# Two attentions with a gate: numerators in halves, inverses sent a head at a time, a tile as the constant, zeros from DRAM

## The chip, the cores and the metric

The kernel runs on one core of one Trainium2 chip. The metric is the device time of one launch in microseconds (us). The kernel before took 1031.26 us, the median of 3 runs (1030.42 to 1031.37). Everything is written for this one shape, and all of it is one launch.

## What is computed

Two attentions over the same 2048 rows of x (448 columns, 16 heads of 28) are mixed by a gate. A is linear attention: a learned feature map with two softmaxes per head, the state kv, the numerators phi_q kv and the denominators phi_q z + 1e-6. B is softmax attention.

```python
# A                                   S = 2048, D = 448, H = 16, Dh = 28
q, k, v = split(x @ A_wqkv)           # heads of 28
pq, pk  = q @ w_phi, k @ w_phi        # per head
phi_q   = concat(softmax(pq), softmax(-pq))        # 56 features; phi_k alike
kv, z   = phi_k.T @ v, sum(phi_k, rows)
num     = phi_q @ kv
den     = (phi_q @ z) + 1e-6
a       = merge_heads(num / den) @ A_wo
# B
b       = merge_heads(softmax(q @ k.T * Dh**-0.5) @ v) @ B_wo
g       = sigmoid((x * gate_w).sum(-1, keepdims=True))
out     = g * a + (1 - g) * b
```

## The kernel before, in words

All sums are kept in float32. A product whose inputs need more than the fast format holds is split into a high and a low part and done in three passes, so that one 128x448 product of 448 inputs is 11 or 12 matmuls on PE. The rows are handled in 16 tiles of 128 (`NT`). The order of the work on PE, DVE, ACT and POOL is written by hand; all the DMAs the text speaks of are issued by one queue, SP, in the order in which they are placed there, and a transfer that has to wait for something holds up all that stand behind it on SP. SP also waits, before each transfer, for the one eight places ahead of it.

The kernel has three stretches. Up to about 176 us, PE computes the projections and the state `KV` of A; from about 346 us to the end it is softmax attention B. Between them lies the part that the change touches: the **loop over q** from 0 to 26, in which A's outputs are made while the values of B are projected. One round holds, in this order and as far as they exist for that q:

- the product `pq` of tile q (lines 116, 11 matmuls), its features (`features1`, `features2`) and their transposition into `fT` (`turn`, line 541, DVE);
- `norm2` early (q = 19), the projection `poa` of `out_a` (line 116, three tiles of 448 columns being 12 matmuls each; ACT scales the result into `ga` at line 593, line 594 stores it to DRAM as `gad`);
- `value_b`, the product `pvb` of a tile of B's values (line 116 or 135, 11 matmuls), at q = 2 to 10, 17 and 22 in this loop;
- at q = 6, 10, 14, 18 the **numerators** `numer(n)` of four tiles together (n = 0 to 3; "tile n" below is such a group of four): 128 matmuls of 32x128 at line 552, each on a quarter of rows and a quarter of columns of PE, from `fT` and `KV` into two PSUM tiles `pn_0` and `pn_1`. Each of these 128 is two matmuls in the trace, each with its weight load. Right behind them, `normalize1` copies both to SBUF (`oUa`, ACT, line 413) and sends the rows that hold the denominators to `dena` (line 418, four DMAs);
- `norm2` at q = 7, 11, 15 late in the round, and at q = 19 early: for each half of the tile DVE adds 1e-6 to `dena` (line 424) and takes the reciprocal (line 425), SP sends it to DRAM as `rda` (line 429, two DMAs for each half), and one DMA for each half spreads it to all 128 partitions, 32 for each of four heads, as `rsa` (line 430, 128 partitions of 1024 numbers, 512 KB);
- `normalize3` (line 436, DVE, numerators times inverses, `oUa` x `rsa`) and `normalize4` (line 444 ACT, high part; line 445 DVE or POOL, low part, `oTa`) three and four rounds after the numerators, which feed `out_a`.

From q = 19 on, single units of B's row maxima are strewn in by `tick` (`mx_unit`: matmuls `pmb` and `pmd` at line 295, then ACT line 302 and DVE line 304). At q = 21 the first operand pair of B is set up in `qk` (the memory of `wqA_s`, whose last use is `pq` of tile 15): POOL sets two stacks of 128x2048 to zero and one row to -1 (lines 873 and 874), then SP loads the transposed queries and keys (line 774, from `qkd`) and the row maxima (line 786, from `nm`). The first scores of B use them (line 960).

Of the kernel before, what the change touches and what calls it, by code (L numbers as in the profile page):

```python
# [17 lines left out]
P = 128  # L18
# [5 lines left out]
NG = 4  # L24
# [11 lines left out]
def f32(ap):  # L36
    return ap.bitcast(F32)
# [3 lines left out]
def gated_mix_kernel(ctx, tc, xT, wqkB, wvB, wvA, wkAT, wqAT, phi, woA, woB,  # L41
# [50 lines left out]
    gate = const.tile([P, NT], F32, name="gate")  # L92
    gate1 = const.tile([P, NT], F32, name="gate1")

    w1p = ctx.enter_context(tc.tile_pool(name="w1p", bufs=1, reuse_waits="tile"))
# [70 lines left out]
    acts = []  # L166
    subs = []
    part = mxp.tile([P, NU * 4], F32, name="part", bufs=1)
    nc.gpsimd.memset(part, LOWEST)
# [251 lines left out]
    def normalize2(pool, oU, den, nm, n, eps):  # L421

        if eps:
            nc.vector.tensor_scalar_add(den, den, EPS)
        nc.vector.reciprocal(den, den)
        rd = dr.tile([4, n * 512], F32, tag=f"rd{n}", name=f"rd{nm}", bufs=2)
        rs = pool.tile([P, n, 512], F32, tag="rs", name=f"rs{nm}", bufs=2)
        for k in range(n):
            nc.sync.dma_start(rd[:, k * 512:(k + 1) * 512], den[:, k, :])
        nc.sync.dma_start(rs.rearrange("p n q -> p (n q)"),  # L430
                          rd.unsqueeze(1).to_broadcast([4, 32, n * 512]))
        return oU, rs
# [110 lines left out]

    def numer(n):

        pn = [ps_mx(f"pn{n}_{i}", False) for i in range(2)] if n else pn_next
        for g in range(NG):
            for b in range(2):
                for a in range(4):
                    for c in range(4):  # L550
                        rows, k = slice(32 * a, 32 * a + DH), 2 * g + b
                        nc.tensor.matmul(pn[a // 2][32 * c:32 * c + 32, a % 2, g * P:(g + 1) * P],  # L552
                                         KV[rows, k // 4, k % 4 * P + 32 * c:k % 4 * P + 32 * c + 32],
                                         fT_of[n][rows, :, 2 * (4 * g + c) + b, :],
                                         start=b == 0, stop=b == 1, tile_position=(32 * a, 32 * c),
                                         skip_group_check=True)
        for i in range(2):
            num[n, i] = normalize1(ta, pn[i], f"a{n}_{i}", 2)
# [133 lines left out]
    for n in range(4, NP):  # L692
# [9 lines left out]
        if n == 14:  # L702
            part_loads("wvA", wvA, 450, "wvA")
            nc.sync.dma_start(sel_s, sel)
            for v in vap:
                nc.gpsimd.memset(v[:, :, 28:32], 0.0)
                nc.gpsimd.memset(v[:, :, 28:29], 1.0)
# [138 lines left out]
    for q in range(NT + 11):  # L846
# [23 lines left out]
        if q == 21:  # L870
            w = f32(weights(1, "qk0"))
            for i in range(2):
                nc.gpsimd.memset(w[:, i], 0.0)
            nc.gpsimd.memset(w[0:1, 1], -1.0)
            qst.append(w[:, 0].bitcast(F32R))
# [17 lines left out]
        if q < NT:  # L893
            fq[q] = features1(pq, f"q{q}", nc.gpsimd)
        norm4(q, "B")
        if 1 < q <= NT:
            fq[q - 1] = features2(fq[q - 1], f"q{q - 1}")
# [3 lines left out]
        for u in ((), (q - 3, q - 2), (q - 2,), (q - 2,))[(q - 2) % 4]:  # L901
            if 0 <= u < NT:
                turn(u)
# [6 lines left out]
        if q == NT + 2:  # L910
            bd_s.close()
            vb = [value_tile(0)]
        norm2(q, True)
        if q >= 11:
            out_a((q - 11) // 4, (q - 11) % 4)
        if q in VALUE:
            value_b(VALUE[q], tick if q > NT + 2 else None)
# [3 lines left out]
        if q % 4 == 2 and 6 <= q <= NT + 2:  # L921
            numer(n4)
        if q == NT + 6:
# [415 lines left out]
```

## Time and profile before

One execution was profiled; it took 1032.88 us, of which the profile's span is 1031.1 us and 1.78 us lie around it.

| | before |
|---|---|
| median of 3 runs | 1031.26 us |
| the profiled execution | 1032.88 us |
| its span | 1031.1 us |
| PE matmul, busy | 1003.3 us (97%) |
| PE weight load, busy | 563.5 us (55%) |
| ACT, busy | 794.6 us (77%) |
| DVE, busy | 679.2 us (66%) |
| POOL, busy | 236.6 us (23%) |
| mean granted PE clock | 0.984 |

Times are us from the start of the span. PE is the matmul stream, PEld the weight loads, SPq the queue of SP. In a timeline a row has the start, the busy time, the engine with line, operation, out<-in, and xN for N instructions in a run; in brackets the idle time before it and what ended it. In the chain of work that ended last a row has start and length; "issue" is time in which the engine waited for nothing that the profile shows. In a table of windows each engine's busy time and count come first, then the granted PE clock, the mean busy share of the 16 DMA engines, and GB/s.

### The profile page before, as it was taken

The page shows a single profiled execution, that of the slowest core. Times are in us where ns is not written, and L with a number is a line of the kernel's source. Part 1 is how long each engine was busy: PE and PEld are TensorE (multiplying, and loading weights), DVE is VectorE, ACT ScalarE, POOL GpSimd, SP SyncE. Part 2 cuts the span into 40 slices and gives each one's busy share as a digit, 9 for nine tenths or more (in the row PEclk, how much of TensorE's full clock was granted, in tenths as well). Part 3 has the DMA queues.
Part 4 walks back from the last instruction along what each step waited for, and adds up shares of the span by engine and source line. Part 5 has one row for each costly group of instructions (what it writes and reads, how often), then busy time and mean ns, then how long its engine had stood idle before and what let it go on. Part 6 is the DMA issues. An engine that isn't in the chain of part 4 may idle for free.

```text
span 1031.1 us, 19220 instructions
## 1 busy us (share of the span) xinstructions
PE 1003.3 (97%) x7116; PEld 563.5 (55%) x7116; DVE 679.2 (66%) x1349; ACT 794.6 (77%) x1491; POOL 236.6 (23%) x230
## 2 busy tenths in 40 slices
PE   9999999999966999999999999999999999999998
PEld 8878777888855643333333333333333444454656
DVE  5567777757754668788878888888887444444202
ACT  5456555444433699999999999999999999979682
POOL 1265455656740420201102101012011011011010
PEclk9999999999987999999999999999999999999999
DMA  8975311512225574223444243352342363316141
GB/s 296 311 249 173 112 59 59 178 44 84 90 82 138 174 169 101 55 63 71 83 94 107 61 93 79 87 107 70 78 94 54 87 137 80 104 36 155 51 120 54
DMA packets 73430, 111.80 MB, mean 108 GB/s; under 512 B 20776, under 2 KB 32728, under 8 KB 73208
## 3 DMA queue, kind: packets, MB, share of 16 engines
q1 hardware_dynamic: 73336, 110.57, 39.8%
q8 instruction: 56, 0.92, 0.4%
q14 instruction: 38, 0.31, 0.1%
HBM read 76.04 MB, written 34.08 MB: 107 GB/s over the span
## 4 chain that ended last, share of the span: by engine, by line
PE 92%; DMA 5%; DVE 2%; issue 1%; SPq 0%; ACT 0%; POOL 0%; POOLq 0%; DVEq 0%; ACTq 0%
PE st L1009 27%; PE pv L1108 24%; PE pm L336 8%; PE pqk L116 6%; PE pq L116 4%; PE pk L135 4%; PE pva L135 4%; PE pob L116 3%; PE pmb L295 2%; PE pvb L116 2%; PE poa L116 2%; DMA qk<-nm 2%; DMA rsa<-rda 1%; PE pvb L135 1%; PE pn L552 1%; DMA kst<-qkd 1%
## 5 line engine op out<-in xcount | busy, mean ns | idle before, releaser
L1012 ACT ACTIVATE p<-st 128x512 f32<-128x512 f32 x1020 | 527.8, 642 | 26.4 <-PE st L1009 26.4
L347 DVE TENSOR_REDUCE part<-pm 128x1 f32<-128x512 f32 x450 | 287.4, 685 | 150.5 <-PE pm L336 150.5
L1108 PE MATMUL pv<-p,vb 128*32 128x512 f32 x2048 | 263.7, 603 | 0.0
L340 ACT ACTIVATE rl<-pm 128x512 f32<-128x512 f32 x200 | 124.6, 623 | 14.1 <-PE pm L336 12.4
L336 PEld LDWEIGHTS pm<-kc,qc 28*128 28x128 f32 x800 | 38.3, 182 | 167.6 <-issue 101.4
L436 POOL TENSOR_TENSOR oUb<-oUb,rsb 128x512 f32<-128x512 f32 x15 | 19.3, 1287 | 460.2 <-DMA rsb<-rdb 196.3
L1009 PE MATMUL st<-qk,kst 128*128 128x512 f32 x384 | 116.2, 425 | 0.6 <-DMA kst<-qkd 0.6
L1009 PE MATMUL st<-qst,kst 128*128 128x512 f32 x384 | 114.8, 423 | 0.0
L344 DVE CUSTOM_DVE_ANT_0 rl<-pm,rl 128x512 f32<-128x512 f32 x150 | 102.0, 680 | 0.0
L336 PE MATMUL pm<-kc,qc 28*128 28x512 f32 x800 | 101.3, 495 | 0.0
L1108 PEld LDWEIGHTS pv<-p,vb 128*32 128x32 f32 x2048 | 47.6, 108 | 95.4 <-issue 88.7
L1009 PEld LDWEIGHTS st<-qst,kst 128*128 128x128 f32 x384 | 64.3, 188 | 37.8 <-ACT p L1012 16.5
L1009 PEld LDWEIGHTS st<-qk,kst 128*128 128x128 f32 x384 | 63.9, 188 | 38.6 <-ACT p L1012 17.8
L304 DVE CUSTOM_DVE_ANT_0 rl<-pmb,rl 128x512 f32<-128x512 f32 x88 | 56.5, 679 | 27.0 <-ACT rl L302 26.9
L302 ACT ACTIVATE rl<-pmd 128x1024 f32<-128x1024 f32 x44 | 45.2, 1027 | 28.6 <-PE pmd L295 20.1
L116 PE MATMUL pqk<-XH,wB 128*128 128x512 f32 x192 | 59.8, 399 | 0.0
L116 PE MATMUL poa<-woA_s,oTa 128*128 128x448 f32 x192 | 48.9, 407 | 2.9 <-ACT oTa L444 2.9
L116 PEld LDWEIGHTS poa<-woA_s,oTa 128*128 128x128 f32 x192 | 39.7, 212 | 9.7 <-ACT oTa L444 3.2
L617 ACT CAST ev<-pqk 128x512 fp32r<-128x512 f32 x28 | 16.1, 588 | 36.5 <-PE pqk L116 29.0
L469 ACT ACTIVATE feat<-feat 128x896 f32<-128x896 f32 x32 | 30.6, 956 | 13.5 <-POOL feat L466 13.5
L116 PEld LDWEIGHTS pqk<-XH,wB 128*128 128x128 f32 x192 | 35.3, 188 | 9.0 <-issue 2.2
L116 PE MATMUL pq<-wqA_s,XH 128*128 128x448 f32 x128 | 39.9, 395 | 0.0
(172 smaller groups left out, 1340.8 us busy)
## 6 DMA issues: line engine op xcount, KB each, us to landing
qkd<-ev SPq DMA_DIRECT2D x28, 512.0 KB
qk<-qkd SPq DMA_DIRECT2D x48, 224.0 KB
kst<-qkd SPq DMA_DIRECT2D x48, 224.0 KB
qst<-qkd SPq DMA_DIRECT2D x32, 224.0 KB
od<-oTb SPq DMA_DIRECT2D x48, 112.0 KB
rsa<-rda SPq DMA_DIRECT2D x8, 512.0 KB
rsb<-rdb SPq DMA_DIRECT2D x15, 256.0 KB
kc<-qkd SPq DMA_DIRECT2D x64, 56.0 KB
```

Source lines behind the costliest of these rows:

```text
L116: nc.tensor.matmul(dst, l, r, start=i == 0, stop=i == len(todo) - 1, skip_group_check=mid is not None)
L135: nc.tensor.matmul(dst[:, :n], l, r, start=i == 0, stop=i == len(todo) - 1, skip_group_check=True)
L302: nc.scalar.activation(rl, pd, AF.Relu)
L304: nc.vector.tensor_tensor_reduce(rl[:, i, :], pb[:, i, :], rl[:, i, :], 1.0, LOWEST, ALU.add, ALU.max, part[:, col + i:col + i + 1])
L336: nc.tensor.matmul(pm[j], mxs[("qc", gq)][js, qt * P:(qt + 1) * P], mxs[("kc", g, kb)][js, :], start=True, stop=True, tile_position=(32 * ...
L340: nc.scalar.activation(rl, pm[kb], AF.Relu if kb < 3 else AF.Copy)
L344: nc.vector.tensor_tensor_reduce(r, pm[j], r, 1.0, LOWEST, ALU.add, ALU.max, part[:, col + j:col + j + 1])
L347: nc.vector.tensor_reduce(part[:, col + j:col + j + 1], pm[j], AX.X, ALU.max)
L469: exps.append(lambda: nc.scalar.activation(fx, fx, AF.Exp))
L1009: nc.tensor.matmul(st, kst_of[(gq // NQ, kt // 4)][:, j, (kt % 4) * P:(kt % 4 + 1) * P], qst_of[gq][:, j, :], start=True, stop=True)
L1012: nc.scalar.activation(p, st, AF.Exp, scale=SCALE)
L1108: nc.tensor.matmul(pv[32 * j:32 * j + 32, :], vb[kt // 8][:, kt % 8, 4 * g + j, :], pt[j], start=kt == 0, stop=kt == NT - 1, tile_position ...
```

## The change

The numerators of a tile are issued in two halves of 64 matmuls (`half` 0 and 1: two of the four groups `g` each), and the first half stands ahead of a value product where one exists in that round; the copy and the loads of the denominators stay behind the second half. The constant 1e-6 is added as a tensor, broadcast from a 128x1 tile `eps_s`. Of the two forms of `normalize2`, the one with two halves (A) sends each inverse row with a DMA of its own, 32 partitions of 1024 numbers, four for what was one. The two stacks are no longer cleared by POOL: a small DRAM tile `c_d` with a row of zeros and a row of -1 is filled early (n = 14 of the first stretch), and five DMAs copy from it, four of them into four partitions each, one into one row. Conditions in the diff that are never true (`2 == 0`, `2 == 1`, `() and`) place nothing; `2 == 2` always holds. In the kernel after, lines are 3 to 12 higher.

```diff
--- before.py
+++ after.py
@@ -91,6 +91,8 @@
     z_s = const.tile([P, NT], F32, name="z_s")
     gate = const.tile([P, NT], F32, name="gate")
     gate1 = const.tile([P, NT], F32, name="gate1")
+    eps_s = const.tile([P, 1], F32, name="eps_s")
+    nc.vector.memset(eps_s, EPS)
 
     w1p = ctx.enter_context(tc.tile_pool(name="w1p", bufs=1, reuse_waits="tile"))
     fr_s = ExitStack()
@@ -165,6 +167,7 @@
     nm_of = {}
     acts = []
     subs = []
+    c_d = dr.tile([2, 4096], F32, tag="cd", name="cd")
     part = mxp.tile([P, NU * 4], F32, name="part", bufs=1)
     nc.gpsimd.memset(part, LOWEST)
     red = mxp.tile([P, 32], F32R, name="red", bufs=1)
@@ -421,14 +424,18 @@
     def normalize2(pool, oU, den, nm, n, eps):
 
         if eps:
-            nc.vector.tensor_scalar_add(den, den, EPS)
+            nc.vector.tensor_add(den, den, eps_s.unsqueeze(1).to_broadcast([P, n, 16]))
         nc.vector.reciprocal(den, den)
         rd = dr.tile([4, n * 512], F32, tag=f"rd{n}", name=f"rd{nm}", bufs=2)
         rs = pool.tile([P, n, 512], F32, tag="rs", name=f"rs{nm}", bufs=2)
         for k in range(n):
             nc.sync.dma_start(rd[:, k * 512:(k + 1) * 512], den[:, k, :])
-        nc.sync.dma_start(rs.rearrange("p n q -> p (n q)"),
-                          rd.unsqueeze(1).to_broadcast([4, 32, n * 512]))
+        if n == 1:
+            nc.sync.dma_start(rs[:, 0, :], rd.unsqueeze(1).to_broadcast([4, 32, 512]))
+            return oU, rs
+        for j in range(4):
+            nc.sync.dma_start(rs[32 * j:32 * j + 32].rearrange("p n q -> p (n q)"),
+                              rd[j:j + 1].to_broadcast([32, n * 512]))
         return oU, rs
 
     def normalize3(oU, rs, n):
@@ -541,10 +548,12 @@
         nc.vector.transpose(fT_of[u // 4][:, u % 4].rearrange("p h t -> p (h t)"),
                             fq.pop(u).rearrange("p h f -> p (h f)"))
 
-    def numer(n):
-
-        pn = [ps_mx(f"pn{n}_{i}", False) for i in range(2)] if n else pn_next
-        for g in range(NG):
+    def numer(n, half):
+
+        if half == 0:
+            num[n] = [ps_mx(f"pn{n}_{i}", False) for i in range(2)] if n else pn_next
+        pn = num[n]
+        for g in (2 * half, 2 * half + 1):
             for b in range(2):
                 for a in range(4):
                     for c in range(4):
@@ -554,7 +563,7 @@
                                          fT_of[n][rows, :, 2 * (4 * g + c) + b, :],
                                          start=b == 0, stop=b == 1, tile_position=(32 * a, 32 * c),
                                          skip_group_check=True)
-        for i in range(2):
+        for i in range(2 * half):
             num[n, i] = normalize1(ta, pn[i], f"a{n}_{i}", 2)
 
 
@@ -702,6 +711,9 @@
         if n == 14:
             part_loads("wvA", wvA, 450, "wvA")
             nc.sync.dma_start(sel_s, sel)
+            nc.vector.memset(gate1, -1.0)
+            nc.sync.dma_start(c_d[0].rearrange("(p n) -> p n", p=P), f32(red))
+            nc.sync.dma_start(c_d[1, :2048].rearrange("(p n) -> p n", p=P), gate1)
             for v in vap:
                 nc.gpsimd.memset(v[:, :, 28:32], 0.0)
                 nc.gpsimd.memset(v[:, :, 28:29], 1.0)
@@ -869,9 +881,10 @@
             pn_next = [ps_mx(f"pn0_{i}", False) for i in range(2)]
         if q == 21:
             w = f32(weights(1, "qk0"))
-            for i in range(2):
-                nc.gpsimd.memset(w[:, i], 0.0)
-            nc.gpsimd.memset(w[0:1, 1], -1.0)
+            for b in range(4):
+                nc.sync.dma_start(w[32 * b:32 * b + 4].rearrange("p i a n -> p (i a n)"),
+                                  c_d[0:1].to_broadcast([4, 4096]))
+            nc.sync.dma_start(w[0:1, 1].rearrange("p a n -> p (a n)"), c_d[1:2, :2048])
             qst.append(w[:, 0].bitcast(F32R))
             kst.append(w[:, 1].bitcast(F32R))
             load_q(0)
@@ -892,14 +905,18 @@
             fq[0] = features2(fq[0], "q0")
         if q < NT:
             fq[q] = features1(pq, f"q{q}", nc.gpsimd)
+        if (2 == 0 or 2 == 3 and q < NT) and q % 4 == 2 and 6 <= q <= NT + 2:
+            numer(n4, 0)
         norm4(q, "B")
+        if () and q % 4 in () and 0 <= q - 2 < NT:
+            turn(q - 2)
         if 1 < q <= NT:
             fq[q - 1] = features2(fq[q - 1], f"q{q - 1}")
         for _ in range({0: 1, 1: 1}.get(q, 0)):
             mx_unit()
         take_subs()
         for u in ((), (q - 3, q - 2), (q - 2,), (q - 2,))[(q - 2) % 4]:
-            if 0 <= u < NT:
+            if 0 <= u < NT and not (q % 4 in () and u == q - 2):
                 turn(u)
         norm4(q, "C")
         if q in (0, 1):
@@ -911,15 +928,19 @@
             bd_s.close()
             vb = [value_tile(0)]
         norm2(q, True)
+        if 2 == 1 and q % 4 == 2 and 6 <= q <= NT + 2:
+            numer(n4, 0)
         if q >= 11:
             out_a((q - 11) // 4, (q - 11) % 4)
+        if (2 == 2 or 2 == 3 and q > NT) and q % 4 == 2 and 6 <= q <= NT + 2:
+            numer(n4, 0)
         if q in VALUE:
             value_b(VALUE[q], tick if q > NT + 2 else None)
         if q == 3:
             kv_out(kvT)
         take_exps()
         if q % 4 == 2 and 6 <= q <= NT + 2:
-            numer(n4)
+            numer(n4, 1)
         if q == NT + 6:
             load_early(0, sum(t < 8 for t in EARLY))
         norm2(q, False)
```

On PE, around the numerators of tile 0 (q = 6). Before, the value product `pvb` stands ahead of all 128 numerator matmuls; the last row of `pq` stands first, and the 16 rows of numerators begin at the end of this piece:

```order
L116 MATMUL pq_2316<-wqA_s,XH 128x448 x2
L116 MATMUL pvb_2339<-wvB_s,XH 128x448 x2
L116 MATMUL pvb_2339<-wvB_s,XL 128x448
L116 MATMUL pvb_2339<-wvB_s,XH 128x448 x2
L116 MATMUL pvb_2339<-wvB_s,XL 128x448
L116 MATMUL pvb_2339<-wvB_s,XH 128x448 x2
L116 MATMUL pvb_2339<-wvB_s,XL 128x448
L116 MATMUL pvb_2339<-wvB_s,XH 128x448 x2
L552 MATMUL pn_0_2233<-fT_2199,KV 32x128 x8
L552 MATMUL pn_1_2234<-fT_2199,KV 32x128 x8
```

After, this is the place where the first half ends, `pvb` stands, and the second half begins:

```order
L561 MATMUL pn_0_2239<-fT_2205,KV 32x128 x8
L561 MATMUL pn_1_2240<-fT_2205,KV 32x128 x8
L118 MATMUL pvb_2409<-wvB_s,XH 128x448 x2
L118 MATMUL pvb_2409<-wvB_s,XL 128x448
L118 MATMUL pvb_2409<-wvB_s,XH 128x448 x2
L118 MATMUL pvb_2409<-wvB_s,XL 128x448
L118 MATMUL pvb_2409<-wvB_s,XH 128x448 x2
L118 MATMUL pvb_2409<-wvB_s,XL 128x448
L118 MATMUL pvb_2409<-wvB_s,XH 128x448 x2
L561 MATMUL pn_0_2239<-fT_2205,KV 32x128 x8
L561 MATMUL pn_1_2240<-fT_2205,KV 32x128 x8
```

The 11 matmuls of `pvb` have moved from ahead of the numerators into their middle, and nothing else on PE has moved there. The same holds for tile 1 (q = 10). For tiles 2 and 3 (q = 14, 18) there is no value product in the round and PE's order is what it was.

On SP, from the inverses of tile 3 to the loads of B's first operands. Before (`gad<-ga` stores an output tile of A; `rda` and `rsa` are the inverses; `qk<-qkd` and `qk<-nm` the operands):

```order
L594 DMA gad_71<-ga_0_3473 128x448
L429 DMA rda_0_3448<-dena_0_3430 4x32x16 x2
L429 DMA rda_1_3455<-dena_1_3435 4x32x16 x2
L774 DMA qk_3515<-qkd 28x4x512
L430 DMA rsa_0_3449<-rda_0_3448 128x1x1024
L430 DMA rsa_1_3456<-rda_1_3455 128x1x1024
L594 DMA gad_71<-ga_1_3512 128x448
L774 DMA qk_3515<-qkd 28x4x512 x3
L786 DMA qk_3515<-nm_1192 1x16x32 x4
L774 DMA qk_3515<-qkd 28x4x512 x4
```

After, with one of the zeroing loads ahead of the inverses (another stands ahead of those of tile 2) and the other three behind them:

```order
L885 DMA qk_3545<-cd 4x4096
L432 DMA rda_0_3472<-dena_0_3454 4x32x16 x2
L432 DMA rda_1_3482<-dena_1_3459 4x32x16 x2
L603 DMA gad_71<-ga_0_3503 128x448
L603 DMA gad_71<-ga_1_3542 128x448
L437 DMA rsa_0_3473<-rda_0_3472 32x1024 x4
L437 DMA rsa_1_3483<-rda_1_3482 32x1024 x4
L885 DMA qk_3545<-cd 4x4096 x2
L887 DMA qk_3545<-cd 1x2048
L786 DMA qk_3545<-qkd 28x4x512 x4
L798 DMA qk_3545<-nm_1198 1x16x32 x4
L786 DMA qk_3545<-qkd 28x4x512 x4
```

The two `rsa` of this tile have become eight, both output stores now stand ahead of them, and all loads of queries behind them. On SP as a whole 695 DMAs have become 726.

## The prediction

> **What bounds the kernel now.** I read the page's busy shares first, then a table of windows.
>
> ```profile
> PE 1003.3 (97%) x7116; PEld 563.5 (55%) x7116; DVE 679.2 (66%) x1349; ACT 794.6 (77%) x1491; POOL 236.6 (23%) x230
> 0.00:176.00 176.00, 174.64 (x1225) 137.95 (x1225) 118.86 (x251) 96.81 (x146) 74.43 (x79) 1.00 0.55 180
> 213.00:346.00 133.00, 111.19 (x1440) 92.06 (x1438) 80.29 (x127) 54.06 (x77) 57.51 (x52) 0.88 0.33 102
> 346.00:1031.00 685.00, 680.47 (x4156) 301.21 (x4152) 451.37 (x922) 624.67 (x1239) 79.76 (x74) 1.00 0.38 89
> ```
>
> The matmul stream is the bound: 97% busy. The one place with slack in it is the stretch 213 to 346 us, which the change edits: 111.19 of 133 us busy, at a granted clock of 0.88. Behind it PE is busy 680.47 of 685 us at clock 1.00, so PE sets the pace there too, and **what PE gains before 346 us should stay to the end**. To see what stops PE I took the chain around the numerators of tiles 0 and 1, and then PE's timeline.
>
> ```profile
> 218.28 1.23 issue
> 220.46 3.99 PE pq L116 x11
> 226.68 2.23 PE pq L116 x11
> 243.48 2.56 issue
> 246.47 3.27 PE pq L116 x11
> ```
>
> ```profile
> 219.51 0.94 PE L552 MATMUL pn<-fT,KV 28*32 28x128 f32 x50 [1.23 <-issue]
> 239.99 3.49 PE L552 MATMUL pn<-fT,KV 28*32 28x128 f32 x246
> 246.04 0.43 PE L552 MATMUL pn<-fT,KV 28*32 28x128 f32 x10 [2.56 <-issue]
> 270.57 1.79 PE L552 MATMUL pn<-fT,KV 28*32 28x128 f32 x102 [1.35 <-issue]
> 292.85 0.90 PE L552 MATMUL pn<-fT,KV 28*32 28x128 f32 x44 [1.74 <-issue]
> 296.70 5.59 PE L116 MATMUL poa<-woA_s,oTa 128*128 128x448 f32 x14 [2.95 <-ACT oTa L444]
> 310.57 0.80 PE L295 MATMUL pmb<-kp,qp 28*128 28x512 f32 x2 [4.32 <-DVE part L304]
> 325.80 0.79 PE L295 MATMUL pmd<-kp,qp 28*128 28x512 f32 x2 [6.33 <-ACT rl_s L302]
> ```
>
> Two kinds of gap are seen. Four, of 1.23 to 2.56 us, stand inside the numerators with no releaser ("issue"). Three, of 2.95, 4.32 and 6.33 us, wait for the normalization of tiles 2 and 3. After a gap the matmuls run slowly for a while: the product `pq` takes 3.99 us after the first and 3.27 us after the second, against 2.23 us.
>
> **Numerators in two bursts.** A tile is 256 matmuls in the trace; the gaps come after 206, 246, 154 and 212 of them (256 less the rows' x50, x10, x102, x44). Counting all of PE's matmuls from gap to gap (the order on PE gives those between) makes 50+88+246 = 384, then 10+44+48+154 = 256, then 102+11+48+11+212 = 384: multiples of 128 pairs of weight load and matmul. I read it as PE's instructions arriving in blocks of 128 pairs (256 instructions): numerators use one up in about 1.8 us (3.49 us for 246), and the next isn't there yet. From the pair where a block ends to the restart I get 3.1 us in tile 0 and 4.3 us in tile 1. The Trainium skill ("Runtime: NRT & Kernel Launch", Instruction fetch mechanics) gives blocks of 256 instructions too, but calls their crossing mostly hidden: by that, the split gains nothing here. The four rows speak against "hidden".
>
> With `pvb` in the middle, tile 0's two block ends lie 39 numerators, 11 value matmuls and 78 numerators apart: 0.6 + 2.23 + 1.1 = 3.9 us, more than 3.1, so this gap should go, and with it the slow `pq`: 1.23 + (3.99 - 2.23) = 3.0 gained. Tile 1 is less lucky: block ends fall on the first numerator of the first half and on the first matmul of `pvb`, only 1.8 us apart, so a stall of 3.1 - 1.8 = 1.3 us (0 to 2.5 by the two refill times) should stay, now ahead of `pvb`. There is a second price: the first half needs the last transposition 2.23 us earlier.
>
> ```profile
> 237.00 1.19 DVE L541 STREAM_TRANSPOSE fT<-feat 128x1024 f32<-128x1024 f32 x1
> 237.82 2.23 PE pvb L116 x11
> 249.74 3.17 PE poa L116 x12
> 255.15 2.46 PE poa L116 x12
> ```
>
> It ends at 238.19, PE could start at 237.82: 0.4 us lost. Tile 1 had 2.56 of gap, 1.04 in `pq` and 0.71 in `poa` (3.17 against 2.46), 4.3 together; with 1.3 and 0.4 kept and a third of the slow clock, I take 2.0. **Together -5.0** (between 0 and -6.9). Tiles 2 and 3 keep their order, and their gaps of 1.35 and 1.74.
>
> **Inverses a head at a time, and the sum.** The path of tile 2 into tile 3, by DVE's, ACT's, POOL's and SP's timelines:
>
> ```profile
> 286.03 1.35 SPq L430 DMA_DIRECT2D rsa<-rda  x2
> 294.77 1.23 DVE L436 TENSOR_TENSOR oUa<-oUa,rsa 128x1024 f32<-128x1024 f32 x1 [6.88 <-DMA rsa<-rda]
> 297.60 1.97 ACT L413 COPY oUa<-pn 128x1024 f32<-128x1024 f32 x2
> 302.34 4.77 DVE L424 TENSOR_SCALAR dena<-dena 128x32 f32<-128x32 f32 x1
> 307.42 1.55 DVE L424 TENSOR_SCALAR dena<-dena 128x32 f32<-128x32 f32 x1
> 309.00 0.35 DVE L425 RECIPROCAL dena<-dena 128x32 f32<-128x32 f32 x1
> 311.10 1.29 SPq L430 DMA_DIRECT2D rsa<-rda  x2
> 322.42 1.23 DVE L436 TENSOR_TENSOR oUa<-oUa,rsa 128x1024 f32<-128x1024 f32 x1 [8.63 <-DMA rsa<-rda]
> ```
>
> The multiplication waits for `rsa` 8.7 us after its issue in tile 2 and 11.3 us in tile 3. Two windows show why, and what a transfer into 32 partitions does (`acc<-gad` is one, 32 partitions each):
>
> ```profile
> 291.00:297.00 6.00, 1.31 (x50) 0.85 (x46) 1.54 (x2) 0.97 (x2) 0.00 (x0) 0.88 0.27 105
> 644.00:647.00 3.00, 3.00 (x22) 1.31 (x18) 2.44 (x5) 2.83 (x7) 0.00 (x0) 1.00 0.99 199
> 640.82 2.36 SPq L1098 DMA_DIRECT2D acc<-gad  x3
> ```
>
> While `rsa` runs, 0.27 of the 16 DMA engines are busy, four of them: 512 KB at 105 GB/s is 5 us, and the second half of the tile queues behind the first. The loads into 32 partitions fill 0.99. The Trainium skill ("DMA: Bandwidth & Descriptors") holds both sides: by its section on the increment by 16 the leading dimension sets the number of engines, here 4 before and 32 after, and the traced shares agree; its rules for authors say that transfers split by partitions only queue up on the same engines, by which the split would gain nothing (the second rival).
>
> For a piece of 128 KB I bound the time from issue to landing by the 11.3 us of the whole from above and from below by 1.9 us, the transfer `rda<-dena` in the chain, and take 2.3 us: 1.9 and 0.4 of data, nearest to that row, since at 199 GB/s the piece is 0.66 us and part of it overlaps.
>
> ```profile
> 284.89 1.91 DMA rda<-dena
> ```
>
> Issues cost SP 0.65 us each (1.35 and 1.29 for two), so the four of a half take 2.6 us. Now step by step, in times of before. Tile 2: issues 286.03 to 288.6, landed at 290.9 at the latest, against 294.77: the multiplication and its cast come 3.9 us earlier, and PE's wait of 2.95 us is gone. The copies of tile 3's numerators start when these end, at 293.75 (292.85 + 0.90) instead of 297.60: also 3.85. So the denominators can be added from 298.5 rather than 302.34. The adds were held until POOL was done:
>
> ```profile
> 303.52 3.55 POOL L873 MEMSET qk<- 128x2048 f32 x2
> 307.13 1.79 POOL L874 MEMSET qk<- 1x2048 f32 x1
> 282.92 0.12 DVE L424 TENSOR_SCALAR dena<-dena 128x32 f32<-128x32 f32 x1
> 296.68 0.69 DVE L445 TENSOR_TENSOR oTa<-oUa,oTa 128x512 fp32r<-128x512 f32 x1 [0.68 <-ACT oTa L444]
> ```
>
> The first add ends at 307.11 and the second at 308.97, as the clearings end (307.07, 308.92); alone it takes 0.12 us. With the clearings gone (5.3 us of POOL) and a tensor as second operand, an add costs between 0.12 and 0.69 us, the latter for 16 times the numbers; I take 0.2, nearest to the first, since it has the same 32 numbers per partition. The last reciprocal ends at 299.6 instead of 309.35. **That is 9.7 us, but SP takes some back**: `rda` goes out at once, yet the store of output tile 1, formerly behind `rsa`, now stands ahead of it and waits for ACT until about 302.4. So `rsa` goes out at 302.95, its fourth piece at 304.9 to 305.5 and it has landed at about 307.0, against 322.42. Multiplication (DVE), cast and `rl_s` (ACT) take the 3.4 us that they took (322.42 to 325.80), so PE goes on at **310.4 instead of 325.80: -15.4**. That includes the 2.95 and 4.32 gaps and leaves some 3 us of the 6.33: PE itself, without gaps and slow clock, is there by 307.5, the bound of what can be had (-18.3).
>
> **Hidden costs.** SP has 31 more issues (24 `rsa`, 5 zero loads, 2 stores), 20 us of its time at 0.65 each. Of these, three zero loads and six `rsa` pieces stand between tile 3's inverses and B's first loads, 6 us.
>
> ```profile
> 314.73 13.21 SPq L786 DMA_DIRECT2D qk<-nm  x4
> 328.05 3.03 SPq L774 DMA_DIRECT2D qk<-qkd  x4
> 361.93 0.63 PE L960 MATMUL st<-qk 128*128 128x512 f32 x2
> ```
>
> The `nm` loads were spread over 13.21 us behind the slow `rsa` (SP's waits put 8.8 us to it); with that gone, 23 issues (8 pieces, 3 zero loads, 12 operands) from 302.95 on end by about 318 instead of 331.1. First scores are at 361.93, 20 us earlier at 341.5: some 20 us of cover. The two early stores and the two fills of constants lie in the first 176 us, where PE is busy 174.64: nothing. Against nothing I set 0.5 us more of regained clock and 0.4 us lost in stores that ACT waits for: the rest is -0.1.
>
> Sum: -5.0 - 15.4 - 0.1 = **-20.5**. The profiled execution's 1032.88 becomes 1012.4; it lay 1.6 us over the median of the runs, so I predict **1011**.
>
> **Rivals.** (1) The gaps in the numerators don't shrink, since a block comes no sooner for a product in between, or tile 0's gap only moves: -15.5, **1016**. For it: the refill times differ (3.1 to 4.3) and tile 1 keeps a block to run dry in. (2) The pieces queue up and a tile's inverses land no earlier than whole: only POOL's hold goes, and of its 9.7 less 3.85 us some 5.9 reach PE, with the numerators **1020**. Against it: 0.99 in the window of the 32-partition loads. (3) No change: a later wait takes the gain back, as if first scores waited for their loads until the old time: **1031**. Against it: 16 us of gain in those loads. (4) Slower: SP becomes the bound. If each of the 23 issues takes 1.7 us instead of 0.65, B's loads end at the first scores (341.5) and PE waits there; the kernel is slower than before from 2.5 us each ((361.9 - 2 - 302.95) / 23). At 2.7, less than the 3.3 that `qk<-nm` had behind `rsa`, the last operand lands at 367, 5 us late: **1036**. Against it: 0.65 for every issue that waits for nothing.
>
> **Chances.** Forecast 0.65 (1004 to 1014), rival 1 0.13, rival 2 0.12, rival 3 0.04, rival 4 0.06. The range takes in the forecast's bounds and the first two rivals: best is -18.3 - 6.9 - 0.5 = -25.7 or 1005.6, and 2 us for slow clock that I didn't price gap by gap; worst is rival 2 at 1020, and 1 us for two adds at 0.69. That leaves a tenth outside. A difference under 0.2% (2 us) can't be told from none; faster by more 0.90, within 0.04, slower 0.06.
>
> **What would show it.** In the profile after: no gap in tile 0's numerators and `pq` behind it at 2.23; a gap of about 1.3 ahead of or in tile 1's `pvb`; `rsa` landing 2 to 3 us after its last issue, at a DMA share far over 0.27; adds under 0.7 us; `qk<-nm` no longer spread; one PE wait of about 3 us for `rl_s` in place of 6.33, and 346 to the end as long as before. A window with a share of 0.27 behind the pieces, or a wait ahead of the first scores, would prove me wrong.

## The result and the profile after

The kernel after took 1019.21 us (median of 4 runs, 1018.57 to 1019.96) where the kernel before took 1031.32: ratio 0.9881, 95% interval 0.9864 to 0.9898, 12.1 us less. 1011 had been predicted, with 1003 to 1021 as the range. The profiled execution took 1018.57 us with a span of 1016.8, 14.3 us less than the one before; it is the fastest of its four, and the steps below are those of the two profiles.

The page's first line and two windows of the kernel after (columns as before; PEclk, DMA share and GB/s are the last three):

```profile
PE 1000.4 (98%) x7116; PEld 560.0 (55%) x7116; DVE 674.6 (66%) x1351; ACT 794.4 (78%) x1491; POOL 232.6 (23%) x227
213.00:346.00 133.00, 122.06 (x1510) 98.71 (x1510) 85.84 (x159) 63.92 (x89) 62.55 (x56) 0.92 0.43 117
346.00:1017.00 671.00, 666.67 (x4082) 291.50 (x4080) 441.09 (x890) 614.79 (x1228) 70.29 (x68) 1.00 0.36 88
```

The stretch that the change edits has less slack (122.06 busy of 133 us, 111.19 before), and the rest is as it was: from the first scores to the end it is 668.7 us (348.09 to 1016.8), before 669.2 (361.93 to 1031.1). So the whole difference lies ahead of the first scores. PE's timeline there:

```profile
235.32 1.91 PE L561 MATMUL pn<-fT,KV 28*32 28x128 f32 x128 [0.44 <-DVE fT L548]
260.43 2.27 PE L561 MATMUL pn<-fT,KV 28*32 28x128 f32 x154
264.10 2.19 PE L561 MATMUL pn<-fT,KV 28*32 28x128 f32 x102 [1.41 <-issue]
288.45 1.36 PE L561 MATMUL pn<-fT,KV 28*32 28x128 f32 x44 [2.36 <-issue]
308.11 0.50 PE L298 MATMUL pmd<-kp,qp 28*128 28x512 f32 x2 [2.43 <-ACT rl_s L305]
322.29 0.62 PE L298 MATMUL pmd<-kp,qp 28*128 28x512 f32 x2 [4.30 <-ACT rl_s L305]
```

Five things are to be seen. The gaps inside the numerators of tiles 0 and 1 are gone, and at tile 1 only the foreseen wait of 0.44 us for the transposition is left. The gaps inside tiles 2 and 3 are there, the second longer than before (2.36 against 1.74). The waits of 2.95 and 4.32 us ahead of tile 3's projections are gone. The wait of 6.33 us for `rl_s` has shrunk to 2.43. And a wait that wasn't there before has come 14 us later: 4.30 us, again for `rl_s`. The chain of work that ended last says what this second wait is:

```profile
302.63 3.72 DMA rsa<-rda
306.37 9.21 DMA qk<-qkd
316.01 4.57 DMA gad<-ga
320.69 0.63 ACT ga L602
321.32 0.92 ACT rl_s L305
322.29 0.62 PE pmd L298 x2
```

The loads of B's operands take 9.21 us of this chain. The stores of two output tiles of A stand behind them on SP and went out at 316.01. ACT, which has two buffers for these output tiles, waited 5.76 us for the store before it could write the next one (`ga`), and `rl_s`, for which PE waits, stands behind `ga` on ACT.

### The profile page after: what moved, and what is told of

The parts are those of the page before. It is cut to its first block, busy times and chain, and to the rows that moved or that the text cites. A ratio compares the mean times of both kernels' runs of the same rounds, so it can differ in the third digit from the quotient of the medians.

```text
span 1016.8 us, 19271 instructions
## 1 busy us (share of the span) xinstructions
PE 1000.4 (98%) x7116; PEld 560.0 (55%) x7116; DVE 674.6 (66%) x1351; ACT 794.4 (78%) x1491; POOL 232.6 (23%) x227
## 4 chain that ended last, share of the span: by engine, by line
PE 95%; DMA 2%; DVE 1%; issue 1%; ACT 0%; SPq 0%; POOL 0%; POOLq 0%; DVEq 0%; ACTq 0%
PE st L1030 28%; PE pv L1129 24%; PE pm L339 9%; PE pqk L118 6%; PE pk L137 4%; PE pva L137 4%; PE poa L118 3%; PE pq L118 3%; PE pob L118 3%; PE pmb L298 2%; PE pn L561 2%; PE pvb L118 2%; PE pvb L137 1%; PE pqk L689 1%; DMA qk<-qkd 1%; PE pkv L503 1%
## 5 line engine op out<-in xcount | busy, mean ns | idle before, releaser
L1144 DVE SCALAR_TENSOR_TENSOR acc<-pob,gate,acc 128x448 f32<-128x448 f32 x12 | 8.2, 684 | 47.3 <-PE pob L118 47.3
```

## The experiments

The theory after the result: the pieces carry the change, the halves give some 6 us up to tile 2, and two things take from it: the zero loads, through that second wait, and half clock behind the gaps that are left. The rivals: that the gain of the halves is swallowed whatever stands behind them; that the pieces count for little beside POOL's hold; that the second wait would come back at another place. Twelve kernels were run in three groups, each group with the kernel before on its chip (medians 1033.34, 1032.99 and 1032.82 us). A ratio is to the kernel before, with the 95% interval.

### One part undone: the halves

```diff
-        if (2 == 2 or 2 == 3 and q > NT) and q % 4 == 2 and 6 <= q <= NT + 2:
-            numer(n4, 0)
...
+            numer(n4, 0)
             numer(n4, 1)
```

> The kernel after, with the numerators of a tile in one piece again behind the value product; the other three parts stay. Theory 1 (the split itself gives what the PE stream shows up to the numerators of tile 2, 6.5 us, and nothing later takes it back, since the chain over tile 3 starts at its numerators): the gaps inside the numerators of tiles 0 and 1 come back and the kernel takes 5 to 7 us more than the kernel after, 1024 to 1026. Theory 2 (the later waits for rl_s, 2.43 and 4.30 us in the kernel after, swallow whatever PE gains before them): 0 to 2 us more, and these two waits shrink by the same amount.

Measured: 1020.29 us, ratio 0.9886 (0.9868 to 0.9905), against 0.9881 and 0.9867 (0.9846 to 0.9889, below) of the kernel after: 0.5 to 2 us for the halves. Theory 2's number; not its reason, since the waits for `rl_s` stayed at 2.26 and 4.64 us. In the profiles, the lead of the kernel after was 5.2 us at the start of tile 2 (260.43 against 265.61), 3.6 at tile 3 (283.03 against 286.67), 1.8 at the first `rl_s` (308.11 against 309.90). Most of it was lost in half clock (stretches at a granted clock of 0.5): behind each of the gaps in tiles 2 and 3 the kernel after ran 6.8 us at half clock, this one 3.4 us.

### One part undone: the pieces

```diff
-        for j in range(4):
-            nc.sync.dma_start(rs[32 * j:32 * j + 32].rearrange("p n q -> p (n q)"),
-                              rd[j:j + 1].to_broadcast([32, n * 512]))
+        nc.sync.dma_start(rs.rearrange("p n q -> p (n q)"),
+                          rd.unsqueeze(1).to_broadcast([4, 32, n * 512]))
```

> The kernel after, with the inverses of a half sent by one DMA again. Theory 1 (the pieces landed early because they are spread over all DMA engines, and this is the largest part of the gain): the whole lands 10 to 13 us after issue in tile 3 at a DMA share of 0.25, PE's wait for rl_s grows from 2.43 to about 8 us, and the kernel takes 5 to 9 us more than the kernel after, 1024 to 1028. Theory 2 (what counted was only that POOL's clearing no longer holds the additions): under 2 us more.

Measured: 1031.41 us, ratio 0.9979 (0.9963 to 0.9994): 10 to 11.5 us more than the kernel after, over theory 1's range, and theory 2 is out. The multiplication of tile 3, with the issue on SP and a window behind it:

```profile
307.94 1.35 SPq L433 DMA_DIRECT2D rsa<-rda  x2
321.45 1.22 DVE L439 TENSOR_TENSOR oUa<-oUa,rsa 128x1024 f32<-128x1024 f32 x1 [14.30 <-DMA rsa<-rda]
```

```profile
318.00:325.00 7.00, 0.19 (x2) 0.19 (x2) 2.12 (x3) 2.30 (x4) 1.08 (x1) 0.50 0.26 92
```

It takes 13.5 us from issue to multiplication, at a share of 0.26; PE's wait for `rl_s` is 14.12 us there.

### One part undone: the zero loads

```diff
-            for b in range(4):
-                nc.sync.dma_start(w[32 * b:32 * b + 4].rearrange("p i a n -> p (i a n)"),
-                                  c_d[0:1].to_broadcast([4, 4096]))
-            nc.sync.dma_start(w[0:1, 1].rearrange("p a n -> p (a n)"), c_d[1:2, :2048])
+            for i in range(2):
+                nc.gpsimd.memset(w[:, i], 0.0)
+            nc.gpsimd.memset(w[0:1, 1], -1.0)
```

> The kernel after, with the stacks cleared by POOL again and no DRAM constants; the addition stays a tensor addition. Theory 1 (the clearing held the addition because of the addition's form, with one tensor operand): the tensor addition takes under 0.7 us beside the clearing, and since three zero loads go from SP's queue the kernel takes 0 to 2 us less than the kernel after, 1017 to 1019. Theory 2 (POOL's clearing holds any work of DVE): the first addition takes 3 to 5 us again and the kernel takes 2 to 5 us more, 1021 to 1024.

Measured: 1011.11 us, ratio 0.9795 (0.9775 to 0.9815): 7.4 to 8.9 us less than the kernel after, where 2 less had been the best expected. It doesn't tell the two theories of the hold apart, since the additions (0.19 us each) were done by 292.95 and the clearing began at 294.30. It shows a cost of the zero loads that neither theory had: the second wait for `rl_s` is 0.29 us instead of 4.30. The windows from 306 to 310 us, first of the kernel after, then of this one:

```profile
306.00:310.00 4.00, 1.89 (x7) 1.50 (x8) 2.29 (x6) 3.61 (x5) 1.30 (x2) 0.86 0.90 109
```

```profile
306.00:310.00 4.00, 4.00 (x12) 3.27 (x13) 3.40 (x9) 1.45 (x2) 0.36 (x2) 0.58 0.93 192
```

Both keep nine tenths of the DMA engines busy, but with the zero loads among the operand loads they move 109 GB/s, without them 192. In the trace the two zero loads that share this time with the operand loads are eight packets of 16 KB, of 1.2 to 2.4 us each. In the chain the operand loads take 6.14 us here, 9.21 there:

```profile
302.48 6.14 DMA qk<-qkd
309.05 5.28 DMA gad<-ga
```

```profile
316.03 0.50 PE L297 MATMUL pmd<-kp,qp 28*128 28x512 f32 x2 [0.29 <-ACT rl_s L304]
```

Counted from the end of tile 3's numerators (288.17 here, 289.81 in the kernel after), the stores go out 5.3 us earlier. Of this 3.1 us lie in the operand loads and the rest ahead of them: without the zero loads one output store stands behind the `rsa` pieces again instead of ahead, and the pieces go out at 296.99 instead of 299.90.

### One part undone: the constant as a tile

```diff
-            nc.vector.tensor_add(den, den, eps_s.unsqueeze(1).to_broadcast([P, n, 16]))
+            nc.vector.tensor_scalar_add(den, den, EPS)
```

> The kernel after, with the constant added as a number again; POOL clears nothing at that time. Both theories of the hold: additions of 0.12 us and no difference, 1018 to 1020. Only if the form costs something without POOL's clearing beside it would this be slower by over 1 us.

Measured: 1015.38 us, ratio 0.9842 (0.982 to 0.9865). That is 2.6 to 4 us under the kernel after, with intervals that overlap; no difference is shown. This kernel and the kernel after have the same order on every engine. What differs in the profiles is the clock. The first half of the stretch from tile 2 to tile 3, in the kernel after, in its second profile (next run), and here:

```profile
258.00:283.00 25.00, 23.59 (x339) 20.46 (x337) 18.11 (x23) 10.50 (x16) 14.61 (x10) 0.86 0.24 70
```

```profile
258.00:283.00 25.00, 23.59 (x346) 20.94 (x345) 19.56 (x25) 10.98 (x17) 16.05 (x12) 0.93 0.29 80
```

```profile
258.00:283.00 25.00, 23.83 (x531) 21.10 (x535) 18.79 (x25) 10.89 (x16) 15.24 (x11) 1.00 0.38 100
```

The clock is 0.86, 0.93 and 1.00 behind the same gap in tile 2, which lasted 1.41, 1.42 and 1.17 us. Up to the first scores, half clock lasts 20.5 us in all in the two profiles of the kernel after and 10.2 us here.

### The kernel after once more

The edit is none.

> The kernel after once more, on the chip of the three runs below. 0.986 to 0.990 of the kernel before. If the length of the half-clock stretches differs from execution to execution (theory 1), its slowest executions have a granted clock at least 0.002 lower than its fastest and lie 2 us or more above them; if they belong to the program (theory 2), all its executions show 0.989 to 0.990.

Measured: 1018.92 us, ratio 0.9867 (0.9846 to 0.9889). Theory 1: its four executions took 1016.33, 1018.2, 1019.64 and 1020.13 us at mean clocks of 0.995, 0.992, 0.990 and 0.990. How long half clock lasts differs from execution to execution of one program, and the times differ with it, by 4 us here.

### The operand loads two rounds later

```diff
-            load_q(0)
-            load_nm(0)
-            load_k(0, 0)
+        if q == 23:
+            load_q(0)
+            load_nm(0)
+            load_k(0, 0)
```

> The kernel after, with B's first operand loads (queries, maxima, keys; not the zeros) placed two rounds later (q = 23), so that the output stores of tile 2 stand ahead of them on SP. Theory 1 (the second wait for rl_s, 4.30 us, is ACT's wait for an output buffer whose store stands behind the loads): that wait is under 1 us and the kernel takes 3 to 7 us less than the kernel after on the same chip, with first scores not waiting. Theory 2 (the transfers as a whole are the limit there, so that another wait takes its place): less than 1.5 us.

Measured: 1016.6 us, ratio 0.9848 (0.9825 to 0.9871), 2 us less than the kernel after, with overlapping intervals. The time lies between what the two theories expected. For the wait it is theory 2: it went to another place. The stores of tile 2 go out early now, the next one stands behind the loads:

```profile
328.81 0.79 PE L298 MATMUL pmd<-kp,qp 28*128 28x512 f32 x2 [4.06 <-ACT rl_s L305]
```

```profile
327.21 0.63 ACT L602 ACTIVATE ga<-poa,z_s 128x448 f32<-128x448 f32 x1 [5.24 <-DMA gad<-ga]
```

So the wait isn't one of place alone: as long as these transfers are slow, some store stands behind them.

### The constant as a tile, alone

```diff
+    eps_s = const.tile([P, 1], F32, name="eps_s")
+    nc.vector.memset(eps_s, EPS)
...
-            nc.vector.tensor_scalar_add(den, den, EPS)
+            nc.vector.tensor_add(den, den, eps_s.unsqueeze(1).to_broadcast([P, n, 16]))
```

> The kernel before with only the constant added as a tensor; POOL still clears the stacks at that time. Theory 1 (the form of the addition, with a number as operand, is what POOL's clearing holds): additions under 0.7 us beside the clearing where they took 4.77 and 1.55, reciprocals done 5 to 6 us earlier, and a gain of 3 to 6 us over the kernel before, since the whole inverses still land late. Theory 2 (any work of DVE is held): additions of 4 us again, no gain.

Measured: 1031.74 us, ratio 0.9996 (0.9976 to 1.0015). For the hold it is theory 1, by DVE's and POOL's timelines:

```profile
301.73 1.30 DVE L426 TENSOR_TENSOR dena<-dena,eps_s 128x32 f32<-128x32 f32 x1
303.33 0.13 DVE L426 TENSOR_TENSOR dena<-dena,eps_s 128x32 f32<-128x32 f32 x1
```

```profile
301.69 1.29 POOL L447 TENSOR_TENSOR oTa<-oUa,oTa 128x512 fp32r<-128x512 f32 x1 [3.03 <-ACT oTa L446]
302.92 3.56 POOL L875 MEMSET qk<- 128x2048 f32 x2
```

The second addition takes 0.13 us in the middle of the clearing; with a number as operand it took 1.55 us there, and the first 4.77. (The first takes 1.30 here, as long as POOL's subtraction beside it.) The reciprocals are done at 303.84 instead of 309.35, 5.5 us earlier, as expected. For the time it is theory 2: no gain. The inverses still go by whole transfers, the second set goes out at 316.40 only, and PE, which goes on at 319.12 instead of 325.80, then waits another 2.51 and 1.44 us for `rl_s` (0.51 and 0.81 before), has 12.8 us of half clock from there on (3.9 before) and its first scores at 361.13 (361.93 before). The Trainium skill ("GPSIMD Engine Reference", 1. Specifications) says that GpSimd's interface to SBUF is shared with VectorE, with contention for DVE instructions in a two-port mode or with two SBUF inputs. For two inputs the clearing doesn't bear this out: the addition with two inputs wasn't held by it. The addition of a number, which has one, was held; whether it ran in a two-port mode no run shows.

### Tiles 2 and 3 split as well

```diff
+        if q >= 11 and q % 4 == 2 and q <= NT + 2:
+            numer(n4, 0)
         if q >= 11:
             out_a((q - 11) // 4, (q - 11) % 4)
```

(on the kernel without zero loads; the first half is no longer placed behind `out_a` for these rounds.)

> The kernel u_zero (the kernel after, stacks cleared by POOL), and the numerators of tiles 2 and 3 are split as well, the 12 matmuls of an output projection standing between the halves. Theory 1 (blocks of PE's instructions arrive too late for a burst of 256 pairs, and each gap can bring half clock): the gaps of 1.49 and 2.41 us in these tiles fall under 0.5 us together, and the kernel takes 3 to 7 us less than u_zero, 1004 to 1008. Theory 2 (later waits swallow it): less than 1.5 us, and the wait for rl_s of 2.88 us grows by what PE gained.

Measured: 1009.99 us, ratio 0.9786 (0.9769 to 0.9802), 1 us less than the kernel without zero loads (0.9795): no difference shown, theory 2's number. The gaps without a releaser are all gone, as theory 1 has it, and other waits stand in their place:

```profile
259.37 1.91 PE L560 MATMUL pn<-fT,KV 28*32 28x128 f32 x128 [0.78 <-DVE fT L547]
280.11 1.90 PE L560 MATMUL pn<-fT,KV 28*32 28x128 f32 x128 [2.28 <-DVE fT L547]
305.30 0.50 PE L297 MATMUL pmd<-kp,qp 28*128 28x512 f32 x2 [3.87 <-ACT rl_s L304]
```

The first halves now wait for the last transposition, 0.78 and 2.28 us, about what the gaps were.

### The pieces alone

The kernel before with the pieces and nothing else (the diff of the second experiment, the other way round).

> The kernel before with one part of the change: each inverse row sent by a DMA of its own. Numerators in one piece, the constant a number, the stacks cleared by POOL. Theory 1 (the pieces carry the change; the additions of tile 3 then come before POOL clears, so that nothing holds them, and no zero loads stand in the way of the stores): 15 to 20 us less than the kernel before, ratio 0.981 to 0.986, better than the whole change. Theory 2 (the additions still run into the clearing and are held to its end): 4 to 9 us less, 0.991 to 0.996, with additions of 3 to 5 us in the trace.

Measured: 1017.52 us, ratio 0.9851 (0.9833 to 0.9868). The gain of 15.3 us is theory 1's: **one part of four gives as much as all four together** (12.1 and 14.1 us; the intervals overlap, so that it gives more isn't shown). The additions of a number take 0.18 us each and are done by 296.97; POOL clears from 298.16 on. There is one wait for `rl_s`, 3.06 us, and no second one.

### The pieces and the halves

The kernel after without its zero loads and with the constant as a number: the diffs of the third and the fourth experiment together.

> As b_rsa, and the numerators of tiles 0 and 1 in halves around the value product: the change without its zero loads and with the constant as a number. Theory 1 (without the stall for output stores, what the halves save reaches the end): 3 to 6 us less than b_rsa, ratio 0.977 to 0.981. Theory 2 (the halves' gain is swallowed later also without that stall): within 1.5 us of b_rsa.

Measured: 1013.5 us, ratio 0.9810 (0.979 to 0.983), 4.0 us less than the pieces alone: theory 1. Without the second wait, the halves' gain reaches the end. This kernel and the one with the constant as a number (0.9842) differ by the zero loads alone: 3.3 us, less than the 7.4 to 8.9 found above, with intervals that overlap.

### The zero loads five rounds earlier

```diff
+        if q == 16:
+            w = f32(weights(1, "qk0"))
+            ... (the five zero loads)
         if q == 21:
-            w = f32(weights(1, "qk0"))
-            ... (the five zero loads)
             load_q(0)
```

> The kernel after with its zero loads placed five rounds earlier (q = 16), when the memory is free; its operand loads move up in SP's queue with them, so that no output store of tile 3 stands behind all of them. Theory 1 (the price of the zero loads is that at 305 us they slow the operand loads, which the stores stand behind): the second wait for rl_s, 4.3 to 4.9 us, is under 1 us and the kernel takes 3 to 9 us less than the kernel after, ratio 0.978 to 0.984. Theory 2 (the zero loads cost wherever they are, or the earlier loads delay the inverses of tile 2 by as much): within 1.5 us of the kernel after, 0.986 to 0.989.

Measured: 1015.67 us, ratio 0.9834 (0.9821 to 0.9848): 3.4 to 4.8 us less than the kernel after. Theory 1, at the lower end of what it expected: the second wait is gone. What remains over the kernel without zero loads (0.9795) lies in tile 3, where the gap inside the numerators is 3.46 us (2.41 there) and the wait for `rl_s` 3.92 (2.88 there).

### Three tiles split

The pieces and the halves, and tile 2 split around its output projection, tile 3 whole.

> As b_rsa_numer, and tile 2's numerators (q = 14) split around an output projection as well; tile 3 stays whole, where the split waited 2.28 us for a transposition. Theory 1: the gap of 1.4 us inside tile 2 becomes a wait of 0.8 us for the transposition ahead of it, and half clock behind it becomes rarer: 1 to 3 us less than b_rsa_numer, 1007 to 1010 where the kernel before takes 1033. Theory 2: no difference beyond 1 us.

Measured: 1010.74 us, ratio 0.9789 (0.9776 to 0.9803), 2.8 us less than the pieces and the halves: inside theory 1's 1 to 3 us, but the intervals overlap, so no difference is shown. With the two kernels at 0.9795 and 0.9786 it is the fastest found; the three can't be told apart. It is faster than the kernel before and the kernel after, though it has neither the tile for the constant nor the zeros from DRAM.

## Why the prediction was right or wrong

The direction and the mechanism of the largest term held, and the time fell into the range; the gain is 0.6 of the forecast's. That the range holds the time is in part luck: the 1004 to 1014 that had been given a chance of 0.65 were missed, and the range reaches 1019 only because it was drawn out to rival 2, which isn't what happened. In the profiles the terms were these.

**Numerators, -5.0 predicted, -6.4 measured** (from the start of the value product or first half, by the chain, to tile 2: 53.83 us before, 47.46 after). Tile 0 went as worked out. The stall of 1.3 us that should have stayed at tile 1 did not come. The step that failed is the time between the two block ends there: "block ends fall on the first numerator of the first half and on the first matmul of `pvb`, only 1.8 us apart". The profile's queue of instructions, in the kernel after as before:

```profile
q8 instruction: 56, 0.92, 0.4%
```

56 packets of 16 KB hold about 254 each of PE's 14,232 instructions (two times 7116), and they can be seen one by one. Around tile 1 they start at 236.74 and 243.34 us before; the second takes 1.27 us, and PE goes on at 246.04, 1.4 us behind its end. After the change they start at 233.27 and 238.22, 5 us apart and not 1.8: the first fetch starts 2 us ahead of the first numerator. I read this as PE taking in its instructions ahead of their execution, so that the block's end was reached while slow products were still being executed; the 1.8 us were the time between two executions, not between two fetches. That the split works because it gives each fetch time agrees with these packets, and the two kernels with more tiles split bear it out: where a tile is split, no gap without a releaser is left. The Trainium skill ("Runtime: NRT & Kernel Launch", Instruction fetch mechanics) says that the next block is fetched while the present one is executed and that the crossing is mostly hidden; for numerators of some 14.6 ns a pair (3.01 us for 206 before) the gaps show that it isn't.

**Inverses and what hangs on them, -15.4 predicted, -11.2 measured** (from tile 2's numerators to the first wait for `rl_s`: 58.85 us before, 47.68 after). The rows that answer to those of before, from DVE and SP:

```profile
281.16 3.64 SPq L437 DMA_DIRECT2D rsa<-rda  x8
285.60 1.23 DVE L443 TENSOR_TENSOR oUa<-oUa,rsa 128x1024 f32<-128x1024 f32 x1 [3.06 <-DMA rsa<-rda]
292.96 0.19 DVE L427 TENSOR_TENSOR dena<-dena,eps_s 128x32 f32<-128x32 f32 x1 [0.41 <-DMA dena<-oUa]
296.00 3.80 SPq L603 DMA_DIRECT2D gad<-ga  x2
299.90 3.62 SPq L437 DMA_DIRECT2D rsa<-rda  x8
304.74 1.22 DVE L443 TENSOR_TENSOR oUa<-oUa,rsa 128x1024 f32<-128x1024 f32 x1 [2.62 <-DMA qk<-cd]
```

From first issue to multiplication it is 4.4 us in tile 2 (8.7 before; 4.9 predicted) and 4.8 in tile 3 (11.3 before; 4.05 predicted). The last row's wait is put to a zero load, but without the zero loads this took 5.6 us (296.99 to 302.58), so they didn't lengthen it. The additions take 0.19 us, as taken. From the end of tile 3's numerators (289.81) to the last reciprocal (294.67) it is 4.9 us, 5.85 predicted, 15.6 before. The stores that wait for ACT stand ahead of the pieces as read from the order, and the pieces go out 0.9 us later behind the numerators' end than predicted. From the numerators' end to PE going on it is 18.3 us, 16.65 predicted, 32.05 before. So 1.65 of the missing 4.2 us lies here, and 2.6 us in tiles 2 and 3 themselves: the gap of tile 3 was 0.6 us longer, half clock behind tile 2's gap lasted 6.8 us instead of 3.4, and behind tile 3's it began early enough to slow the last 44 matmuls (1.36 us against 0.90). The same stretch took 45.9 us in the second profile of the kernel after and 42.3 in the one with the constant as a number, where no half clock fell into it; predicted were 43.45. The size is right where the clock stays full; for the clock the prediction had only 2 us in its range.

**Hidden costs, -0.1 predicted, +3.9 measured** (first wait for `rl_s` to first scores: 36.1 us before, 40.0 after, 41.8 in the second profile). This is the step that failed: "0.5 us more of regained clock and 0.4 us lost in stores that ACT waits for". The cover was measured for the loads themselves, and held: first scores never waited. But the stores stand behind those loads on SP, ACT behind the stores, PE behind ACT, and there the cover is not 20 us but the 2 buffers of `ga`. Rival 4 had SP as the bound by the time of its issues, with PE waiting ahead of the first scores; the issues took less than foreseen (3.62 us for eight, 0.45 each instead of 0.65), and no wait came there. The size of the failed term shows in the stretch from the first wait for `rl_s` to the first scores: of the kernels with pieces it takes 40.0 to 41.8 us in the five profiles with zero loads beside or just ahead of the operand loads, and 34.3 to 35.1 in the six without them or with them five rounds earlier. So the zero loads there cost 5 to 7.5 us instead of nothing: they slow the operand loads (9.2 instead of 6.1 us) and let them start later, and half clock follows the wait. Undoing them alone removes the second wait, moving them earlier removes it too, moving the operand loads only moves it. The kernels' medians give 3.3 to 8.9 us for them; the stretch ahead, from tile 2 to that first wait, differs by more than 5 us among these profiles (42.3 to 47.7), in the main by its half clock. That zero loads slow the transfers beside them is measured as GB/s; why 16-KB rows into four partitions do so wasn't tried.

**The rivals.** Gaps that don't shrink (1016) and pieces that land no earlier (1020) lie near the measured time, and neither is what happened. The Trainium skill's rule ("DMA: Bandwidth & Descriptors", Rules for kernel authors) that transfers to two halves of the partitions aren't worth it speaks of halves that each go over all the engines already. It doesn't fit this kernel, where the whole kept 0.26 of the engines busy and the pieces 0.92, and the split gave 15 us. That it is the number of leading rows, 32 in a piece and 4 in the whole, agrees with these shares; the rows alone were not changed in any run.

## What to carry to other kernels

A change of several parts is to be costed part by part on the chip: here one part gave 15 us, one 4, one none that could be shown, and one took 3 to 9 back. The cover of an added transfer is not the time until its own reader, but the shortest one among all that stand behind it on its queue, and an engine with two output buffers has little. Where PE is the bound, gaps of one or two microseconds can cost more than their length, by the half clock that may follow.

## What the runs showed of the hardware

- A gap of 1.1 to 3.5 us inside PE's stream was followed by none, 3.4 or 6.8 us at half clock, differing between executions of one program (6.8 and 3.4 us behind gaps of 1.41 and 1.42 us in the two profiles of the kernel after). From the restart in tile 2 to tile 3 PE took 15.97 us without half clock, 17.42 with 3.4 us of it and 18.93 with 6.8: 3 us lost. Executions of the kernel after differ by 4 us with mean clocks of 0.995 to 0.990.
- Clearing by POOL held DVE's addition of a number (4.77 and 1.55 us for 0.12) and not its addition of a tensor (0.13 us). Not held either was the custom operation of the row maxima, 0.69 us beside the clearing as elsewhere, in the kernel without zero loads.
- With one DMA of 4 rows spread to 128 partitions for each half, 0.27 of the DMA engines were busy; with four DMAs of 32 partitions each, 0.92. This is a window of the kernel after over the pieces of tile 2, in which a store and the load `vd` ran as well:

```profile
281.00:286.00 5.00, 5.00 (x223) 4.25 (x221) 1.65 (x2) 0.23 (x1) 0.26 (x1) 1.00 0.92 276
```
